# Background work paced by what is needed, a two-part weave of layers 0 and 1, and unread matmuls in the gaps

## The chip, the core and the metric

The kernel runs on one core of a Trainium2 chip. TensorE (PE) multiplies, and its weight loads (PEld) are shown as a row of their own; ScalarE (ACT) applies functions such as exp; VectorE (DVE) works elementwise; GpSimd (POOL) does small jobs; SyncE (SP) issues the DMAs. The metric is the device time of one execution in microseconds, lower is better. Before the change the median of 7 runs is 2521.17 us (2514.41 to 2530.74).

## The reference

Four attention layers follow each other on 2,048 tokens of width 640, with 32 heads of 20. Layers 0 and 2 (weights A) look back over a window of 256 keys, layers 1 and 3 (weights B) over all keys:

```python
def _A_ref(x, wqkv, wo):                     # _B_ref: the same without the mask
    q, k, v = split_heads(x @ wqkv)          # 32 heads of 20
    scores = einsum("bhqd,bhkd->bhqk", q, k) * (Dh ** -0.5)
    mask = (i - j >= 0) & (i - j < 256)
    p = softmax(where(mask, scores, -1e9))
    return merge_heads(einsum("bhqk,bhkd->bhqd", p, v)) @ wo

x = A_x
x = x + _A_ref(_layernorm(x), A_wqkv, A_wo)
x = x + _B_ref(_layernorm(x), B_wqkv, B_wo)
x = x + _A_ref(_layernorm(x), A_wqkv, A_wo)
x = x + _B_ref(_layernorm(x), B_wqkv, B_wo)
```

## The kernel before, in words

The tokens are cut into four chunks of 512 queries (`c`), the heads into eight groups of four (`g`). A *unit* is the attention of one layer, chunk and group. Its scores are made in *banks*: 128 keys by 512 queries of one head, which fill one PSUM bank. A full unit has 64 banks (16 blocks of keys, four heads), a windowed one 12. A *tile* is two or three banks, and the main loop goes through the tiles of all units in the order of the list `units`. For tile `t` it emits:

1. the score matmuls on TensorE (L790), 32 rows each, into one of two PSUM buffers of three banks, so that four heads' strips can run side by side;
2. exp on ScalarE (L804), which writes `pt`;
3. background work, by `pump` (L203);
4. the mask for tile `t-1` on VectorE (L828), in windowed units;
5. the value matmuls (L843) for four banks of two or three tiles earlier, 21 columns of weights each, summed in bank 7 (`op`). At a unit's end VectorE copies `op` away (L668) and a *tail* divides by the sum of the softmax (L685 to L718).

Tiles of units that `narrow` names (layer 0, and the "a" parts of layer 1) alternate between three and two banks, all others have three. While there are narrow units (`state["early"]`) background work has two PSUM banks, 5 and 6; after that only bank 6.

Background work is everything else: layer norm and its transposes (`t_ln`), values (`t_v`), queries and keys (`t_qk_window` for layers 0 and 2, `t_qk_full` for 1 and 3), the output projection (`t_out`). These are Python generators in a list `todo`, sorted by the unit that first needs them. Each yields the cost of what it has just emitted, in *credits*, which are meant as microseconds of TensorE: 0.22 for a matmul of 512 columns, 0.14 for one of 320. A projection is five such matmuls, an output item eight; once begun, an item is emitted whole (`"hold"`), even if credit turns negative, and then nothing is emitted until credit is above zero. Tails come before everything and don't wait for credit. `pump` adds 1.2 credits a tile in layer 0 and 0.6 later, and keeps at most 1.0.

If a unit starts and something it needs isn't made, `require` (L233) emits it at once, however long it takes. The order of instructions on every engine is thus fixed when the program is built; TensorE, ScalarE, VectorE and SyncE each run theirs in that order.

Layers 1 and 3 keep queries, keys and values in DRAM. A projection is evacuated into `st` by VectorE (by ScalarE while `state["act"]`, that is in layer 0), stored, and loaded again as `kt`, `vt`, `qt` by `load_unit` (L592), one unit ahead where its needs are ready. The weights of a group's query and key, padded to 32 rows a head, are one tile `wqk` (320 KB), loaded by `get_w` from DRAM for each chunk, with one load ahead (`take_w`).

The units of layer 1, chunk 0 are cut in "a" (key blocks 0 to 11) and "b" (12 to 15) for the first three groups; part "a" leaves its sum in `raw_o`, and "b" adds to it. They follow all of layer 0. Later, the windowed units of layer 2 are woven between the full units of layers 1 and 3, and layer 3's chunk 0 is cut in the same way for all eight groups.

Of the kernel before, what the change touches and what calls it, by code (L numbers as in the profile page):

```python
# [9 lines left out]
BF16 = mybir.dt.bfloat16  # L10
# [4 lines left out]
P = 128  # L15
# [12 lines left out]
VW = DH + 1  # L28


@with_exitstack
def kernel(
# [19 lines left out]
    wqkp = pool("wqkp", 4)  # L52
# [101 lines left out]
    class Task:  # L154
# [4 lines left out]
        def __init__(self, name, gen, need):  # L159
            self.name, self.gen, self.need, self.wake = name, gen, need, 0  # L160
            self.holds = False
            Task.count += 1
            self.key = (need, Task.count)
# [4 lines left out]
    def push(name, gen, need):  # L168
        insort(todo, Task(name, gen, need))

    def push_tail(name, gen):
        tails.append(Task(name, gen, 0))
# [4 lines left out]
    def advance(task):  # L177
        state["running"] = task
        try:
            kind, n = next(task.gen)  # L180
        except StopIteration:
            drop(task)
            state["held"] = None
            return 0.0
        state["held"] = task if kind == "hold" else None
        if kind == "wait":
            task.wake = state["tick"] + n
            return 0.0
        return n
# [13 lines left out]
    def pump(credit):  # L203
        state["credit"] = min(state["credit"] + credit, 1.0)
        while True:
            t = choose(state["credit"] <= 0.0)
            if t is None:
                break
            state["credit"] -= advance(t)
# [36 lines left out]
    cap = {"qa": 3, "ka": 18, "va": 10, "xnT": 5, "kt": 3, "vt": 3, "qt": 4, "ln": 1, "w": 2, "vs": 2}  # L246

    def room(*tags):
        while any(live[t] >= cap[t] for t in tags):
            yield ("wait", 1)  # L250
        for t in tags:
            live[t] += 1
        state["running"].holds = True
# [16 lines left out]
    worder = {0: [], 1: [], 2: [], 3: []}  # L270

    def get_w(w, g, first):
        t = wqkp.tile([P, 2, KD, P], BF16, name="wqk", tag="wqk")
        if first:
            tv = t[:].rearrange("p n c (j m) -> p (n c) j m", j=4)
            nc.gpsimd.memset(tv[:, :, :, DH:32], 0.0)
            for n in range(2):
                src = raw[:, :, n * D + 80 * g : n * D + 80 * (g + 1)]
                nc.vector.tensor_copy(
                    out=t[:, n].rearrange("p c (j m) -> p c j m", j=4)[:, :, :, 0:DH],  # L280
                    in_=src.rearrange("p c (j e) -> p c j e", j=4),
                )
            nc.sync.dma_start(out=wqk_d[w][g], in_=t[:].rearrange("p n c m -> p (n c m)"))
        else:
            nc.sync.dma_start(out=t[:].rearrange("p n c m -> p (n c m)"), in_=wqk_d[w][g])
        return t

    def push_proj(key, l, w, g, gen, need, first=False):
        worder[l].append((key, w, g, first))
        push(key, gen, need)  # L290

    def take_w(key, l):
        yield from room("w")
        order = worder[l]
        i = next(n for n, e in enumerate(order) if e[0] == key)
        if key not in wtiles:
            wtiles[key] = get_w(*order[i][1:])
            if not order[i][3]:
                yield ("wait", 4)
        i = next(n for n, e in enumerate(order) if e[0] == key)  # L300
        order.pop(i)
        wt = wtiles.pop(key)
        if i < len(order) and not any(e[0] in wtiles for e in order):
            wtiles[order[i][0]] = get_w(*order[i][1:])
        return wt
# [8 lines left out]
    def project(wt, n, xt, dst):  # L314
        mb = yield from take_m()
        pq = ps[:, mb, :]
        for dc in range(KD):
            nc.tensor.matmul(  # L318
                pq, lhsT=wt[:, n, dc, :], rhs=xt[:, dc, :],
                start=(dc == 0), stop=(dc == KD - 1),  # L320
            )
            if dc < KD - 1:
                yield ("hold", 0.22)
        evac(dst(), pq)
        drop_m(mb)
        yield ("pe", 0.22)
# [14 lines left out]
    def t_ln(l, c):  # L341
# [3 lines left out]
        users[l, c] = 10 if l == 1 else 9  # L345
# [95 lines left out]
    def t_qk_window(key, l, c, g):  # L441
        while ("xnT", l, c) not in ready:
            yield ("wait", 1)
        yield from room("qa", "ka")
        wt = yield from take_w(key, l)
        q = qap.tile([P, C], BF16, name="qa", tag="qa")
        yield from project(wt, 0, xnT[l, c], lambda: q[:])
        k = kap.tile([P, C], BF16, name="ka", tag="ka")
        yield from project(wt, 1, xnT[l, c], lambda: k[:])
        live["w"] -= 1  # L450
        qa[c, g], ka[c, g] = q, k
        used(l, c)
        ready.add(("qk", l, c, g))

    def t_qk_full(key, l, c, g):

        while "prep_b" not in ready:
            yield ("wait", 1)
        while ("xnT", l, c) not in ready:
            yield ("wait", 1)  # L460
        wt = yield from take_w(key, l)
        for n, dst in ((1, k_d[l][:, g, c * C : (c + 1) * C]), (0, q_d[l][:, c, g, :])):
            yield from project(wt, n, xnT[l, c], staged)
            nc.sync.dma_start(out=dst, in_=staging.pop())
        live["w"] -= 1
        used(l, c)
        ready.add(("qk", l, c, g))
# [36 lines left out]
    def push_layer(l, c):  # L504

        need = [first_use(l, c, g) for g in range(G)]
        push(("ln", l, c), t_ln(l, c), need[0])
        if l == 1:
            push(("v", l, c, 0), t_v(l, c, (0,)), need[0])
            push(("v", l, c, 1), t_v(l, c, (1,)), need[4])  # L510
        else:
            push(("v", l, c), t_v(l, c, (0, 1)), need[0])
        for g in range(G):
            key = ("qk", l, c, g)
            if l % 2:
                push_proj(key, l, 1, g, t_qk_full(key, l, c, g), need[g])
            else:
                push_proj(
                    key, l, 0, g, t_qk_window(key, l, c, g), need[g], first=(l == 0 and c == 0)
                )  # L520


    class Unit:
        def __init__(self, l, c, g, part=None):
            self.l, self.c, self.g, self.part = l, c, g, part
            self.windowed = l % 2 == 0
            if self.windowed:
                sets = [(m, b0, subs, j) for m, b0, subs in window_banks(c) for j in range(4)]
            else:
                kcs = {None: range(NT), "a": range(12), "b": range(12, NT)}[part]  # L530
                sets = [(None, 0, [(kc, 0, 4, 0)], j) for kc in kcs for j in range(4)]
            n = len(sets)
            self.banks = [
                (self, j, m, b0, subs, i < 4, i >= n - 4, i == n - 1)
                for i, (m, b0, subs, j) in enumerate(sets)
            ]
# [33 lines left out]
    units = [Unit(0, c, g) for c in range(NC) for g in range(G)]  # L570
    units += [Unit(1, 0, g, "a") for g in range(3)]
    units += [Unit(1, 0, g, "b" if g < 3 else None) for g in range(G)]
# [12 lines left out]
    def first_use(l, c, g):  # L585

        if l % 2 == 0:
            return index[l, c, g, None]
        keys = [(l, 0, g, "a" if c < NC - 1 else "b"), (l, 0, g, None)]
        return next(index[k] for k in keys if k in index)  # L590

    def load_unit(u):  # L592
# [3 lines left out]
        k0, k1 = {None: (0, NT), "a": (0, 12), "b": (12, NT)}[u.part]  # L596
# [13 lines left out]
    def unit_needs(u):  # L610
# [3 lines left out]
        chunks = range(NC - 1) if u.part == "a" else range(NC)  # L614
        return [n for cc in chunks for n in (("qk", l, cc, g), ("v", l, cc, g // 4))]
# [69 lines left out]
    def t_tail(l, c, g, on, oT):  # L685
# [36 lines left out]
        if g == G - 1:  # L722
            need = first_use(l + 1, c, 0) if l < 3 else len(units) + c
            push(("out", l, c), t_out(l, c), need)
# [8 lines left out]
    def t_prep_b():  # L733
# [5 lines left out]
        for g in range(G):  # L739
            get_w(1, g, True)  # L740
            yield ("wait", 4)
        ready.add("prep_b")

    with tc.manual_schedule():
        push("stats", t_stats0(0), 0)
# [9 lines left out]
        tiles = []  # L755
        n = 0
        while n < len(banks):
            size = 2 if len(tiles) % 2 and narrow(banks[n][0]) else 3
            tiles.append(banks[n : n + size])
            n += size  # L760

# [3 lines left out]
        for t in range(len(tiles) + 8):  # L765
            state["tick"] += 1
            n_b = 0
            if t < len(tiles):
                cur = tiles[t]
                n_b = len(cur)  # L770
                for b in cur:
                    u = b[0]
                    if id(u) not in started:
                        started.add(id(u))
                        if u.l == 0 and u.g == 0 and u.c + 1 < NC and u.c not in pushed:
                            pushed.add(u.c)
                            push(("stats", u.c + 1), t_stats0(u.c + 1), index[0, u.c + 1, 0, None])
                            push_layer(0, u.c + 1)
                            if u.c == 0:
                                push("prep_b", t_prep_b(), index[0, 1, G - 1, None])  # L780
                        state["unit"] = index[u.l, u.c, u.g, u.part]
                        state["act"] = u.l == 0
# [29 lines left out]
                pump(1.2 if cur[0][0].l == 0 else 0.6)  # L812
            else:
                pump(2.0)
# [37 lines left out]
        while tails or todo:  # L852
            state["tick"] += 1
            pump(5.0)
# [30 lines left out]
```

The softmax here doesn't subtract the row's maximum and nothing guards it: scores larger than these inputs give would overflow.

## Time and profile before

| | before |
|---|---|
| median of 7 runs | 2521.17 us (2514.41 to 2530.74) |
| the profiled execution | 2521.89 us |
| its span, first to last instruction | 2520.2 us |
| TensorE clock granted, mean | 0.736 of full |
| exp on ScalarE, L804 | 1,688 instructions, 2198.6 us busy |
| score matmuls, full units, L790 | 4,096, 716.9 us busy |
| value matmuls, full units, L843 | 4,096, 535.6 us busy |
| query and key projections, L318 | 1,280 issued, 347.8 us busy |
| output projections, L482 | 1,024, 179.6 us busy |
| DMA queue of SyncE | 150.64 MB, 19.3% of 16 engines |

The busy table gives for each engine the time in which it had an instruction, its share of the span and the number of instructions. The row PEclk cuts the span in 40 equal slices (63 us each) and gives the clock that TensorE was granted, in tenths of full speed. The sums by stretch give the same busy times for a chosen window. The chain of waits follows the work that ended last back in time: start, length, what. In the timeline a row is a run of like instructions on one engine; brackets give the idle time before it and what ended it. A matmul's shape such as `32*128 32x512` is rows and columns of weights, then the moving operand.

### The profile page before, as it was taken

Reading aid. Unit: us, or ns where it says so; the run is one execution under the profiler, and the core shown is the slowest. Engines: PE = TensorE matmul, PEld = TensorE weight load, DVE = VectorE, ACT = ScalarE, POOL = GpSimd, SP = SyncE. Lnnn points to the kernel's source line nnn. Section 1 sums busy time; section 2 is a strip of 40 time slices with the busy share of each in tenths; the row PEclk is TensorE's granted clock in tenths of the full one; section 3 lists DMA queues with packets and bytes.
Section 4 is the critical chain, followed back from the end, with each engine's and each line's share of the span. In section 5 each row is a group of like instructions: output and inputs, shape, how many; then the busy total and the mean of one; then the engine's idle time right before and its main releaser. Section 6 shows DMA issues by size and latency. Waiting matters only on the chain.

```text
span 2520.2 us, 37403 instructions
## 1 busy us (share of the span) xinstructions
PE 2060.3 (82%) x15313; PEld 731.5 (29%) x15424; DVE 852.6 (34%) x1925; ACT 2264.8 (90%) x1831; POOL 48.3 (2%) x113
## 2 busy tenths in 40 slices
PE   6788987887878898779987888888877787778777
PEld 3334432322322233223332233233322222222222
DVE  6686842321323334334343434643200010001001
ACT  6778866989998999899999989899999999999995
POOL 2000000000000000000000000000000000000000
PEclk9899998885866699757896589868755565556555
DMA  5212133332210132002231033104211010011100
GB/s 163 70 59 63 46 101 100 112 105 68 66 53 17 42 101 97 29 33 51 79 95 43 1 84 97 62 18 117 79 35 49 32 43 32 33 43 48 32 17 11
DMA packets 92893, 153.03 MB, mean 61 GB/s; under 512 B 8881, under 2 KB 59057, under 8 KB 92721
## 3 DMA queue, kind: packets, MB, share of 16 engines
q1 hardware_dynamic: 92720, 150.64, 19.3%
q8 instruction: 120, 1.97, 0.3%
q14 instruction: 53, 0.43, 0.1%
HBM read 120.46 MB, written 30.15 MB: 60 GB/s over the span
## 4 chain that ended last, share of the span: by engine, by line
ACT 47%; PE 28%; issue 14%; DVE 9%; DMA 1%; SPq 0%; ACTq 0%; POOL 0%; DVEq 0%
ACT pt L804 47%; PE ps L318 9%; PE ps L790 6%; PE ps L843 4%; PE ps L405 4%; PE ps L482 4%; DVE pt L828 3%; DVE oT L668 1%; PE ps L369 1%; DVE st L266 1%; DMA wqk<-wqk_d 1%; DVE on L718 1%; DMA qt<-q_d 1%; DVE qa L266 1%; DVE x_sb L490 1%
## 5 line engine op out<-in xcount | busy, mean ns | idle before, releaser
L804 ACT ACTIVATE pt<-ps 128x1536 bf16<-128x1536 f32 (+1 forms) x1688 | 2198.6, 1532 | 188.5 <-PE ps L790 170.3
L790 PE MATMUL ps<-qt,kt 32*128 32x512 bf16 x4096 | 716.9, 507 | 300.6 <-ACT pt L804 267.2
L843 PE MATMUL ps<-pt,vt 128*21 128x512 bf16 x4096 | 535.6, 509 | 6.0 <-DVE oT L668 4.4
L790 PEld LDWEIGHTS <-kt 32*128 32x128 bf16 x4096 | 204.5, 95 | 771.4 <-issue 738.2
L318 PE MATMUL ps<-xnT,wqk 128*128 128x512 bf16 x1169 | 347.8, 416 | 33.5 <-DMA wqk<-wqk_d 7.4
L828 DVE TENSOR_TENSOR pt<-pt,masks 128x1024 bf16<-128x1024 bf16 (+5 forms) x403 | 240.0, 625 | 215.2 <-ACT pt L804 214.8
L668 DVE CAST oT<-ps 128x512 bf16<-128x512 f32 x117 | 80.3, 686 | 505.4 <-PE ps L843 505.0
L843 PEld LDWEIGHTS <-vt 128*21 128x21 bf16 x4096 | 106.1, 91 | 331.8 <-issue 327.7
L482 PE MATMUL ps<-wop,on 128*128 128x320 bf16 x1024 | 179.6, 324 | 10.3 <-DVE x_sb L490 5.1
L318 PEld LDWEIGHTS <-wqk 128*128 128x128 bf16 x1280 | 116.0, 103 | 190.6 <-issue 102.1
L790 PE MATMUL ps<-qa,ka 32*128 32x384 bf16 (+2 forms) x1408 | 133.6, 320 | 31.2 <-ACT pt L804 28.7
L266 DVE CAST st<-ps 128x512 bf16<-128x512 f32 x119 | 82.3, 692 | 208.3 <-PE ps L318 207.9
L490 DVE TENSOR_TENSOR x_sb<-x_sb,ps 128x320 bf16<-128x320 bf16 x128 | 62.0, 484 | 187.0 <-PE ps L482 184.4
L482 PEld LDWEIGHTS <-on 128*128 128x128 bf16 x1024 | 98.1, 104 | 78.7 <-issue 38.0
L405 PE MATMUL ps<-wv,xnT 128*128 128x320 bf16 x640 | 115.2, 319 | 6.6 <-DVE vs L266 2.1
L718 DVE TENSOR_TENSOR on<-oT,ps 128x512 bf16<-128x512 bf16 x128 | 87.6, 684 | 87.9 <-PE ps L714 86.7
L843 PE MATMUL ps<-pt,va 128*21 128x384 bf16 (+2 forms) x1408 | 88.2, 318 | 18.8 <-DVE oT L668 18.1
L695 DVE RECIPROCAL rz<-ps 128x16 f32<-128x16 f32 x128 | 32.8, 257 | 156.5 <-PE ps L690 147.5
L405 PEld LDWEIGHTS <-xnT 128*128 128x128 bf16 x640 | 58.8, 102 | 51.1 <-issue 29.7
L790 PEld LDWEIGHTS <-ka 32*128 32x128 bf16 x1408 | 39.5, 96 | 116.9 <-issue 110.9
L714 PE MATMUL ps<-rT,spread 32*128 32x128 bf16 x512 | 63.1, 256 | 3.2 <-DVE rT L707 2.3
L369 PE MATMUL ps<-ident,xn 128*128 128x128 bf16 x320 | 36.5, 262 | 25.5 <-DVE xn L360 22.6
(50 smaller groups left out, 646.5 us busy)
## 6 DMA issues: line engine op xcount, KB each, us to landing
wqk<-wqk_d SPq DMA_DIRECT2D x120, 320.0 KB
kt<-k_d SPq DMA_DIRECT2D x53, 512.0 KB
vt<-v_d SPq DMA_DIRECT2D x53, 336.0 KB
qt<-q_d SPq DMA_DIRECT2D x75, 128.0 KB
k_d<-st SPq DMA_DIRECT2D x64, 128.0 KB
q_d<-st SPq DMA_DIRECT2D x64, 128.0 KB
v_d<-vs SPq DMA_DIRECT2D x16, 336.0 KB
wqk_d<-wqk SPq DMA_DIRECT2D x16, 320.0 KB
```

Source lines behind the costliest of these rows:

```text
L266: nc.vector.tensor_copy(out=out_, in_=in_)
L318: nc.tensor.matmul(pq, lhsT=wt[:, n, dc, :], rhs=xt[:, dc, :], start=(dc == 0), stop=(dc == KD - 1),)
L405: nc.tensor.matmul(pv, lhsT=xt[:, dc, i * P : (i + 1) * P], rhs=wv_sb[l % 2][:, dc, h * HD : (h + 1) * HD], start=(dc == 0), stop=(dc == K ...
L482: nc.tensor.matmul(yp, lhsT=on[:, g, qb * P : (qb + 1) * P], rhs=wop[:, g, i * HD : (i + 1) * HD], start=(g == 0), stop=(g == G - 1),)
L490: nc.vector.tensor_tensor(out=xv, in0=xv, in1=yp, op=ALU.add)
L668: nc.vector.tensor_copy(out=oT[:], in_=op)
L714: nc.tensor.matmul(zb[:, qb * P : (qb + 1) * P], lhsT=spread4[:, qb, :], rhs=rT[:], start=True, stop=True,)
L718: nc.vector.tensor_tensor(out=on[:, g, :], in0=oT[:], in1=zb, op=ALU.mult)
L790: nc.tensor.matmul(sp[:, i, col * P : (col + qn) * P], lhsT=u.k(kc, j), rhs=u.q(j, q0, qn), start=True, stop=True,)
L804: nc.scalar.activation(out=pt[:, i:k, b0 * P :], in_=sp[:, i:k, b0 * P :], func=ACT.Exp, scale=SCALE,)
L828: nc.vector.tensor_tensor(out=pt_[:, i:k, b0 * P :], in0=pt_[:, i:k, b0 * P :], in1=mv_, op=ALU.mult,)
L843: nc.tensor.matmul(op[32 * j : 32 * j + VW, q0 * P : (q0 + qn) * P], lhsT=u.v(kc, j), rhs=pt[:, i, col * P : (col + qn) * P], start=(first ...
```

## The change

- Layer 1's chunk 0 is cut for all eight groups, with "a" as key blocks 0 to 7 and "b" as 8 to 15 (`SPLIT`). The first four "a" units are woven between the windowed units of layer 0, chunk 3; the other four follow, then the eight "b". Layer 3 is cut as before.
- Query and key are separate tasks in layers 1 and 3, each with its own need: keys by the part that reads them, queries by the unit of their own chunk. The weights are loaded as halves (160 KB), nine buffers in place of four.
- `state["act"]` ends with layer 0's chunk 2: from chunk 3 on VectorE evacuates.
- `pump` gets a rate. In layer 0, chunks 0 to 2, it is 1.2 as before. After that `rate` takes the largest, over the tasks in hand, of the credits left up to a task divided by the tiles until 16 before its unit, at least 0.6 while early and 0.35 after, times 1.1, at most 0.9. Credit is kept up to the rate and 0.1.
- After the early part and until unit (3, 1, 0) starts, `keep_clock` spends credit that is left on matmuls of the identity with a mask, 128 rows by 512 columns, into bank 6; nothing reads them. The built program has 268 of them.

```diff
+SPLIT = {1: 8, 3: 12}
...
-    wqkp = pool("wqkp", 4)
+    wqkp = pool("wqkp", 9)
...
-    def pump(credit):
-        state["credit"] = min(state["credit"] + credit, 1.0)
+    def pump(credit, most):
+        state["credit"] = min(state["credit"] + credit, most)
...
-    def t_qk_full(key, l, c, g):
+    def t_full(l, n, c, g):
...
-        wt = yield from take_w(key, l)
-        for n, dst in ((1, k_d[l][:, g, c * C : (c + 1) * C]), (0, q_d[l][:, c, g, :])):
-            yield from project(wt, n, xnT[l, c], staged)
-            nc.sync.dma_start(out=dst, in_=staging.pop())
+        yield from room("w")
+        wt = yield from take_w(l, n, c, g)
+        yield from project(wt, xnT[l, c], staged)
+        dst = k_d[l][:, g, c * C : (c + 1) * C] if n else q_d[l][:, c, g, :]
+        nc.sync.dma_start(out=dst, in_=staging.pop())
...
+    def keep_clock():
+
+        while state["held"] is None and state["credit"] > 0.2:
+            b = min(mfree, key=mfree.get)
+            if mfree[b][0] > state["tick"]:
+                return
+            nc.tensor.matmul(
+                ps[:, b, :], lhsT=ident[:], rhs=masks[:, 0, :], start=True, stop=True
+            )
+            state["credit"] -= 0.22
...
-    units = [Unit(0, c, g) for c in range(NC) for g in range(G)]
-    units += [Unit(1, 0, g, "a") for g in range(3)]
-    units += [Unit(1, 0, g, "b" if g < 3 else None) for g in range(G)]
+    units = [Unit(0, c, g) for c in range(NC - 1) for g in range(G)]
+    for g in range(G):
+        units.append(Unit(0, NC - 1, g))
+        if g % 2 == 0:
+            units.append(Unit(1, 0, g // 2, "a"))
+    units += [Unit(1, 0, g, "a") for g in range(G // 2, G)]
+    units += [Unit(1, 0, g, "b") for g in range(G)]
...
+        def rate(t):
+
+            u = tiles[t][0][0]
+            if u.l == 0 and u.c < NC - 1:
+                return 1.2
+            done, r = 0.0, 0.6 if state["early"] else 0.35
+            for task in todo:
+                done += max(task.left, 0.0)
+                if task.need < len(units):
+                    r = max(r, done / max(starts[id(units[task.need])] - t - 16, 1))
+            return min(1.1 * r, 0.9)
...
-                        state["act"] = u.l == 0
+                        state["act"] = u.l == 0 and u.c < NC - 1
...
-                pump(1.2 if cur[0][0].l == 0 else 0.6)
+                r = rate(t)
+                pump(r, r + 0.1)
+                if not state["early"] and state["unit"] < index[3, 1, 0, None]:
+                    keep_clock()
```

## The prediction

> **What bounds the kernel now.** I read the busy table and the row of granted clocks first, then the sums by stretch, then the chain of waits where ScalarE stands still.
>
> ```profile
> span 2520.2 us, 37403 instructions
> PE 2060.3 (82%) x15313; PEld 731.5 (29%) x15424; DVE 852.6 (34%) x1925; ACT 2264.8 (90%) x1831; POOL 48.3 (2%) x113
> PEclk9899998885866699757896589868755565556555
> ```
>
> ScalarE's exp is the bound: 90% busy, and idle time on it is the only time to be won. TensorE's clock is at half speed in much of the second part. Three stretches in the sums (columns: length; busy time and count for PE, PEld, DVE, ACT, POOL; granted clock; DMA share and GB/s):
>
> ```profile
> 260.00:320.00 60.00, 54.25 (x571) 25.40 (x577) 48.71 (x115) 51.45 (x60) 4.07 (x7) 1.00 0.18 53
> 318.50:341.60 23.10, 12.76 (x69) 6.25 (x69) 9.60 (x20) 2.22 (x3) 0.38 (x1) 0.84 0.44 135
> 952.00:1006.00 54.00, 47.09 (x390) 17.56 (x393) 22.02 (x42) 52.37 (x39) 0.00 (x0) 1.00 0.33 108
> 1876.00:2038.00 162.00, 126.42 (x777) 33.74 (x774) 12.52 (x35) 162.00 (x122) 0.00 (x0) 0.50 0.12 38
> ```
>
> In the last one ScalarE never stops although the clock is 0.50: 40 score tiles take 53.7 us there, 1.343 us each, the floor. In the first (layer 0, chunk 3) PE is nearly full. In the second ScalarE does nothing for 21 us. The chain of waits tells why (start, length, what):
>
> ```profile
> 324.83 2.30 DMA k_d<-st
> ...
> 328.24 3.31 DMA wqk<-wqk_d
> 331.55 0.45 issue
> 331.99 3.32 PE ps L318 x9
> 335.32 0.02 issue
> 335.34 0.70 DVE st L266
> ...
> 337.40 3.57 DMA qt<-q_d
> 340.96 0.04 issue
> 341.01 0.29 PE ps L790
> ```
>
> The first unit of layer 1 asks for keys of chunk 2 that are not made: weights are waited for, projected, evacuated, stored, loaded back. Elsewhere what costs time is background work met by a half clock. The timeline of ScalarE and of TensorE where a chunk's output projection begins:
>
> ```profile
> 1812.76 5.65 ACT L804 ACTIVATE pt<-ps 128x1536 bf16<-128x1536 f32 x4 [1.41 <-PE ps L790]
> 1809.39 2.31 PE L482 MATMUL ps<-wop,on 128*128 128x320 bf16 x8
> 1812.58 1.26 PE L482 MATMUL ps<-wop,on 128*128 128x320 bf16 x8
> ```
>
> The same eight matmuls take 2.31 us cold and 1.26 us warm, and the cold ones cost exp 1.41 us. Over the trace, full three-bank tiles that carry one item (five or eight wide matmuls, about 1.1 credit) last 2.705 us on average at half clock (19 tiles), 1.470 us at full clock (156), against 1.343 with none. So a cold item costs 1.36 us, a warm one 0.13. About 24 items ran cold from end to end and as many partly.
>
> **What sets the clock.** [...] By the trace what counts is wide matmuls (128 rows, 128 columns of weights): clock changes come in steps of 3.41 us, and of the windows with under 1,200 wide columns 361 of 367 were followed by half clock, with 2,000 to 4,000 columns 220 of 225 by full clock; the switch is near 1,400. [...] 0.385 credit a tile (0.35 times 1.1) is some 890 columns a tile, 2,270 a window: enough if spread evenly. Items are not: one is issued whole (2,560 columns), then credit is negative for two or more tiles.
>
> **Up to the end of layer 0 and the early parts.** Before's tile 254 and after's tile 263 close the same work (657 and 661 banks, 237 and 235 credits of background), so I compare up to there. Before it ends at 498 us.
> - Stalls. ScalarE's gaps at 341.6 and 344.5 (20.9 and 1.9 us) and at 387.7, 424.2, 441.0, 451.1 (5.7, 4.5, 8.1, 2.3) sum to 43.4. The later three belong to "b" units whose keys are made at the moment of use. In the changed order every full unit but the first of layer 1 has its needs made six or more tiles ahead, so these go. The first still asks at its start, for 11 wide matmuls: 2.4 us warm, up to 3.3 for weights, 5.7 for evacuation, store and load as above, less one tile of cover: +10. Weights now come as halves, and eight of those loads are used within one tile of their place in the order (none within two tiles before); I estimate 1 us each, the 2.4 to 3.8 us that TensorE waits for a weight load issued at its use (at 332 and 384 us) less the lead, and half of them fall here: +4. Net -29.
> - Windowed tiles of chunk 3. They take 1.9 us (tiles 120 to 150) with 1.2 credit each and evacuations on ScalarE behind each item. Afterwards 0.67 credit and evacuation on VectorE. Bounds: 1.13 (exp alone) and 1.9; the row nearest is 1.55 at 0.57 credit in chunk 0. I take 1.5: 33.6 tiles x 0.4 = -13. The 26 evacuations moved (about 0.45 us each of ScalarE) are inside this. VectorE takes them at 0.69 us; it was at 48.7 of 60 us there, so this gain is partly at its mercy.
> - Where that work goes: 102 two-and-three-bank "a" tiles at 1.25 us (1.19 at 0.57 credit before) and 7 full ones at 1.41, 138 us, against 58 at 1.2 and 43 at 1.41, 130 us: +8.
> - Before tile 120 the changed order does 5.5 more credits and stops once for 11 matmuls (layer 0, chunk 2, group 4): +8.
>
> Sum: -26.
>
> **From there to the end.** 1,403 tiles in 1,997 us, of which 123 lie above the floor.
> - Spacing of items. The distance to the item before is one or two tiles for 171 of 233 items before and 105 of 236 after; three tiles for 4 and 61; more for the rest (57 and 69). A burst at 0.6 warms the clock with its first item and pays once; at 0.385 each comes alone. Laying both orders on 1.34 us tiles and 3.41 us windows gives 51 items cold or half cold before (the trace's own number) and 63 after, with 23 and 40 cold throughout. 17 more at 1.36: +22. The bounds: none cold (about -50), or all the 61 at distance three (+76).
> - Unread matmuls: 268 in 152 tiles, from tile 338 to 1118. Warm they cost nothing: a tile's own passes take 0.56 us (0.32 for scores, three in four tiles 0.32 for values, from the starts of such passes around 960 us), two more matmuls 0.43, inside 1.343. Cold, they are 0.85 on top of 0.95 (0.54 a pass at 1942 us): about 0.25 a tile too much; a quarter of the tiles would be cold: +8. If all were: +38.
> - Fewer cold tiles with small pieces: -4. Gone: 6.3 us at 1498 (first "a" unit of layer 3) and 4.8 at 1571 (a weight load); new late halves +4: together -7.
> - Layer 3's output projections after (3,1,0) have no unread matmuls and the slower rate; they are in the count of items.
> - The DMAs move the same bytes in twice as many weight transfers (240 for 120). All are issued by SP, at 20% DMA share, ahead of the stores that follow them: nothing, given leads of four tiles or more.
>
> Sum: +19. Exp itself is unchanged (2,161 us before and after by the same rates; 7 more tiles).
>
> Together -7 on a span of 2520.2. The profiled execution took 2521.9 and the median is 2521.2, so I predict **2514 us** for the median.
>
> **Rivals.**
> - A, as worked out: early gain and later loss nearly cancel, 2490 to 2538.
> - B, the clock is held. For: 2,270 columns a window on average. Against: the empty tiles after each item. Then some 40 of the 51 cold items become warm, 1.24 each, -50; with -4, -7 and -26: 2434.
> - C, the other side: items that come alone run cold. A three-tile distance is 4.0 us, longer than a 3.41 us window, and a tail between two makes it five tiles. From A's 63 on, six more cold items at 1.24 bring the time back to that of before; half of the 61 give 2552, all of them 2590. Against: at exactly three tiles a warm item still leaves half of itself in every window.
> - D, the stall only moves: VectorE, with masks and evacuations of chunk 3 in one queue, holds the windowed tiles at 1.9, and late weight halves cost more than 1 us. Then the early gain is about 8 and the time 2532.
>
> **How the numbers follow.** A measurement tells 0.3% (7.6 us) from no change. A 0.44, B 0.11, C 0.27, D 0.18. A gives 0.22 faster, 0.15 same, 0.07 slower; B 0.11 faster; C 0.02 faster, 0.02 same, 0.23 slower; D 0.02, 0.04, 0.12. Faster 0.37, same 0.21, slower 0.42. To hold 8 in 10 the range takes in A and the nearer half of B and of C: 2462 to 2565.
>
> **What would show it.** Right: no exp gap over 12 us after the first 100 us; gaps at 387 to 451 gone; the granted clock near 1.0 in slices that hold the unread matmuls, and 0.5 to 0.8 where items and tails alternate; mean clock above 0.736, about 0.78; exp gaps of 1 us and more behind a cold item, one by one, from 500 us on, some 50 of them. Wrong: a middle part with mean clock above 0.95 and hardly a gap (B); tile times over 1.5 us throughout 640 to 1500 us (C); windowed tiles of chunk 3 at 1.9 us (D); or PE waits for weights of over 3 us more than a few times.

## The result, and the profile after

The changed kernel takes 2515.12 us in the median of 14 runs (2507.45 to 2519.26), beside 2521.17 of the kernel before in 33 runs on the same chip: ratio 0.9969, 95% interval 0.9957 to 0.9982. The profiled execution took 2514.28 us, with a span of 2512.6. The lines of the page of the changed kernel that answer to those shown of before, with the group of exp (L845) and that of the unread matmuls (L533; the trace has records of 235 of the 268):

```profile
span 2512.6 us, 38178 instructions
PE 2048.6 (82%) x15550; PEld 739.3 (29%) x15692; DVE 868.7 (35%) x1956; ACT 2252.5 (90%) x1812; POOL 48.6 (2%) x129
PEclk9899899988898898879888799889765575557556
...
L845 ACT ACTIVATE pt<-ps 128x1536 bf16<-128x1536 f32 (+2 forms) x1695 | 2197.7, 1509 | 192.2 <-PE ps L831 172.5
...
L533 PE MATMUL ps<-masks,ident 128*128 128x512 bf16 x235 | 86.3, 431 | 3.0 <-issue 1.9
```

Exp is still the bound (ScalarE 90% busy) and its own time is unchanged, 2197.7 us for 2198.6. The clock row is higher in its middle, and from slice 31 on nearly what it was. Cut at the same place as in the prediction (before's tile 254, now tile 263), the traces say:

| end of, us | before | after | difference |
|---|---|---|---|
| tile 120 | 256.8 | 259.8 | +3.0 |
| tile 254 / 263 (early part) | 497.9 | 486.6 | -11.3 |
| last exp | 2494.9 | 2489.1 | -5.8 |

So the early part gained 11 us and the rest gave 6 back. Forecast were 26 and 19: the difference of the two was right, neither of the two was. The early part of the kernel before, with the same instructions, ended at 497.9, 499.2 and 502.0 us in three executions (the second and third from runs 4 and 12 below), and that of the changed kernel at 486.6 to 494.5 in four; over these the gain is about 10.

**Where the early gain went.** TensorE's waits from 256 to 500 us (what waited, for what: us in total, times, longest), first in the kernel before, then in the changed one:

```profile
PE ps L790 <- DMA qt<-q_d: 16.3, 4, 5.4
...
PE ps L318 <- DMA wqk<-wqk_d: 6.3, 2, 3.6
```

```profile
PE ps L318 <- DMA wqk<-wqk_d: 18.6, 7, 5.8
...
PE ps L831 <- DMA qt<-q_d: 5.7, 1, 5.7
```

Score matmuls (L790, now L831) wait for loaded queries once instead of four times, as forecast. But projections (L318) wait seven times for halves of weights, where they waited twice for whole ones. The chain of waits around the longest of these waits (start, length, what; L109 loads weights of an output projection, in four parts), and exp's row in the timeline behind it (brackets: idle before, and what ended it):

```profile
421.95 0.31 SPq L109
...
423.50 6.95 DMA wqk<-wqk_d
430.45 0.05 issue
430.50 0.61 PE ps L318
```

```profile
433.46 2.37 ACT L845 ACTIVATE pt<-ps 128x1536 bf16<-128x1536 f32 x2 [6.92 <-PE ps L831]
```

The half's load is issued right behind the four loads, when its projection is already next, and takes 6.95 us to land, where the two other halves shown here take 2.73 and 3.82. From 421.95 to 430.5 us the DMA engines are 69% busy, at 147 GB/s. TensorE waits 5.78 us for it and exp stands still for 6.92. The chain around the second longest shows why a load can be issued so late:

```profile
461.69 0.59 DVE st L269
462.28 1.97 DMA k_d<-st
464.24 0.02 issue
464.26 0.02 SPq L628
464.28 0.03 issue
464.31 0.32 SPq L628
464.62 0.05 issue
464.68 0.42 SPq L630
465.10 0.05 issue
465.15 0.42 SPq L466
465.57 0.04 issue
465.62 0.43 SPq L287
...
468.20 3.82 DMA wqk<-wqk_d
472.02 0.05 issue
472.06 2.31 PE ps L318 x5
```

In this chain SP issues one transfer behind the other, from 464.31 to 468.20 us. At the head of its queue stands the load of a unit's keys (L628), which waits for the landing of the store of the last of them. SP's own waits from 456 to 475 us:

```profile
SPq L466 <- DVE st L269: 2.0, 1, 2.0
SPq L628 <- DMA k_d<-st: 2.0, 2, 1.1
```

This wait is the one of 1.1 us. Before it SP had stood 2.0 us for an evacuation that a store needs, and 0.9 for the landing of an earlier store. Behind the load of the keys (0.32 us) seven transfers are issued one after another, at 0.42 to 0.49 us each, ahead of the half of the weights that TensorE needs next. That half is issued at 468.20, 3.9 us after the keys. TensorE waits 5.34 us, and exp's gap is 7.18.

**The first "a" unit** asks at its start, as the prediction said, at 263 us:

```profile
263.22 2.73 DMA wqk<-wqk_d
265.95 0.45 issue
266.39 1.93 PE ps L318 x4
268.32 0.02 issue
268.35 0.70 DVE st L269
269.05 0.02 issue
269.06 1.70 DMA k_d<-st
270.76 0.02 issue
270.78 0.32 SPq L628
271.10 0.05 issue
271.15 2.72 DMA qt<-q_d
```

Weights, projection, evacuation, store and load follow one another, and exp's gap that ends at 274.7 is 14.88 us. The gap had begun at 259.8: until the weight load is issued, the chain runs through VectorE's steps of a tail (257.81 to 262.83).

**The rest.** Sums by stretch, from 498 to 1500 and from 1500 to 2490 us, before first and then after (length; busy time and count of PE, PEld, DVE, ACT, POOL; clock; DMA share and GB/s):

```profile
498.00:1500.00 1002.00, 832.24 (x6247) 295.44 (x6293) 351.16 (x775) 928.57 (x705) 10.95 (x30) 0.75 0.20 59
1500.00:2490.00 990.00, 801.70 (x5470) 251.81 (x5487) 195.54 (x440) 959.39 (x712) 3.65 (x10) 0.63 0.16 49
```

```profile
498.00:1500.00 1002.00, 831.45 (x6481) 304.93 (x6547) 360.89 (x802) 926.25 (x704) 10.91 (x30) 0.86 0.20 60
1500.00:2490.00 990.00, 794.06 (x5457) 250.27 (x5481) 190.75 (x431) 953.56 (x706) 3.65 (x10) 0.66 0.15 46
```

In the first of them the clock rose from 0.75 to 0.86, and exp's share didn't rise with it (928.57 and 926.25 us busy of 1002). Tile by tile, with the time above exp's floor of 1.343 us a full tile and the clock around the tile (cold: half speed throughout; part: some of it), from the early part's end on. Windowed tiles count by their columns:

| us above the floor (number of tiles) | before | after |
|---|---|---|
| tiles with an item, cold | 38 (27) | 48 (34) |
| tiles with an item, part cold | 27 (21) | 24 (21) |
| tiles with an item, warm | 27 (187) | 35 (181) |
| tiles with unread matmuls | none | 11 (152) |
| small pieces and all others | 33 | 13 |
| sum | 124 | 132 |

Items lose 108 us instead of 92.

### The profile page after: what moved, and what is told of

Same layout as the page of the kernel before. It is cut to its first block, busy times and chain, and to the rows that moved or that the text cites. A ratio compares the mean times of both kernels' runs of the same rounds, so it can differ in the third digit from the quotient of the medians.

```text
span 2512.6 us, 38178 instructions
## 1 busy us (share of the span) xinstructions
PE 2048.6 (82%) x15550; PEld 739.3 (29%) x15692; DVE 868.7 (35%) x1956; ACT 2252.5 (90%) x1812; POOL 48.6 (2%) x129
## 4 chain that ended last, share of the span: by engine, by line
ACT 42%; PE 31%; issue 15%; DVE 9%; DMA 2%; SPq 0%; POOL 0%; another core or an unknown queue 0%; ACTq 0%; DVEq 0%
ACT pt L845 41%; PE ps L318 10%; PE ps L831 7%; PE ps L887 5%; PE ps L484 4%; DVE pt L872 3%; PE ps L405 3%; DMA wqk<-wqk_d 1%; PE ps L533 1%; DVE st L269 1%; PE ps L739 1%; DVE oT L693 1%; PE ps L369 1%; DVE x_sb L492 1%; DVE on L743 1%
## 5 line engine op out<-in xcount | busy, mean ns | idle before, releaser
L845 ACT ACTIVATE pt<-ps 128x1536 bf16<-128x1536 f32 (+2 forms) x1695 | 2197.7, 1509 | 192.2 <-PE ps L831 172.5
L831 PE MATMUL ps<-qt,kt 32*128 32x512 bf16 x4096 | 680.9, 481 | 285.4 <-ACT pt L845 266.8
L887 PE MATMUL ps<-pt,vt 128*21 128x512 bf16 x4096 | 504.0, 478 | 14.1 <-DVE oT L691 4.6
L831 PEld LDWEIGHTS <-kt 32*128 32x128 bf16 x4096 | 197.1, 94 | 727.4 <-issue 708.4
L318 PE MATMUL ps<-xnT,wqk 128*128 128x512 bf16 x1171 | 357.7, 426 | 46.0 <-DMA wqk<-wqk_d 21.3
L872 DVE TENSOR_TENSOR pt<-pt,masks 128x1024 bf16<-128x1024 bf16 (+6 forms) x403 | 239.2, 625 | 148.3 <-ACT pt L845 148.0
L318 PEld LDWEIGHTS <-wqk 128*128 128x128 bf16 x1280 | 118.7, 105 | 215.2 <-issue 114.3
L831 PE MATMUL ps<-qa,ka 32*128 32x384 bf16 (+2 forms) x1408 | 116.8, 282 | 32.4 <-ACT pt L845 28.5
L533 PE MATMUL ps<-masks,ident 128*128 128x512 bf16 x235 | 86.3, 431 | 3.0 <-issue 1.9
L831 PEld LDWEIGHTS <-ka 32*128 32x128 bf16 x1408 | 40.3, 92 | 101.2 <-issue 94.3
```

What stands on the lines that cost most here:

```text
L318: nc.tensor.matmul(pq, lhsT=wt[:, dc, :], rhs=xt[:, dc, :], start=(dc == 0), stop=(dc == KD - 1),)
L533: nc.tensor.matmul(ps[:, b, :], lhsT=ident[:], rhs=masks[:, 0, :], start=True, stop=True)
L831: nc.tensor.matmul(sp[:, i, col * P : (col + qn) * P], lhsT=u.k(kc, j), rhs=u.q(j, q0, qn), start=True, stop=True,)
L845: nc.scalar.activation(out=pt[:, i:k, b0 * P :], in_=sp[:, i:k, b0 * P :], func=ACT.Exp, scale=SCALE,)
L872: nc.vector.tensor_tensor(out=pt_[:, i:k, b0 * P :], in0=pt_[:, i:k, b0 * P :], in1=mv_, op=ALU.mult,)
L887: nc.tensor.matmul(op[32 * j : 32 * j + VW, q0 * P : (q0 + qn) * P], lhsT=u.v(kc, j), rhs=pt[:, i, col * P : (col + qn) * P], start=(first ...
```

## The experiments

Diffs are against the changed kernel, in runs 4 and 12 against the kernel before and in run 10 against run 9. A kernel's ratio is always to the kernel before, timed beside it, with its 95% interval. "Early end" is the end of tile 254 or 263 in the profiled execution. The same early instructions ended at 486.6, 494.5, 490.5 and 488.8 us in four executions, so one trace doesn't place 4 us. Unread matmuls write a bank that the next item overwrites, so with and without them the same is computed.

**1. The unread matmuls taken out.**

```diff
                 pump(r, r + 0.1)
-                if not state["early"] and state["unit"] < index[3, 1, 0, None]:
-                    keep_clock()
```

> The changed kernel without its 268 unread matmuls; nothing else moves, and the output is the same. Theory (items that come alone pay, the unread matmuls give about what they take): some 20 more items run cold from end to end, 25 us, and the 10 us that the unread matmuls cost in cold tiles, with the cold tiles around them, come back: 2505 to 2535 us, mean clock down from 0.79 to about 0.75. Rival B (the unread matmuls are what pays in this change): over 2540 us.

Measured: 2518.89 us (2514.21 to 2522.82), 0.999 [0.9975, 1.0006]. With the 268 unread matmuls it was 2515.12, so they seem to gain about 4 us; the two intervals overlap, and that is not clear of noise. Without them the clock from 498 to 1500 us falls from 0.86 to 0.79. In the two traces the rest is 2001.0 us without and 2002.5 with them, so a single pair of traces doesn't show where the 4 us lie.

**2. Bursts as before, on the new order, without unread matmuls.**

```diff
-                r = rate(t)
-                pump(r, r + 0.1)
-                if not state["early"] and state["unit"] < index[3, 1, 0, None]:
-                    keep_clock()
+                pump(1.2 if cur[0][0].l == 0 and cur[0][0].c < NC - 1 else 0.6, 1.0)
```

> The changed kernel's weave, separate query and key tasks and half weights, but background work paced as before (1.2 credits a tile in layer 0 up to chunk 2, then 0.6, at most 1.0 kept), and no unread matmuls. Theory (the rate of 0.385 spreads the items over single tiles where each pays for a cold clock): bursts return, the items cold from end to end fall from 34 to about 25, and the gain of the weave stands alone: 2470 to 2500 us. Rival (the pacing is what helps, the weave alone brings stalls): over 2515 us.

Measured: 2504.78 us (2498.59 to 2510.12), 0.9936 [0.9915, 0.9957]: 14 us faster than run 1, and between the two forecasts. Runs 1 and 2 differ in the rate and in the credit kept: up to layer 0's chunk 2 only in the credit kept (1.0 here, 1.3 in run 1), behind it in both. By the traces the gain lies in the early part (479.2 for 494.5; the changed kernel's own early part ends at 486.6 to 494.5, so 7 to 15 us), and the rest is equal (2004.0 and 2001.0, items losing 106 us in both). The edit changes the release of work in both parts, so this pair cannot speak for the spacing of items in the rest. Run 12 was made for that.

**3. Unread matmuls in every tile with no item.** Two of them wherever a tile has no wide work, regardless of credit: 750 for 268.

```diff
-        while state["held"] is None and state["credit"] > 0.2:
+        if state["held"] is None and state.get("wide") != state["tick"]:
             b = min(mfree, key=mfree.get)
...
-            nc.tensor.matmul(
-                ps[:, b, :], lhsT=ident[:], rhs=masks[:, 0, :], start=True, stop=True
-            )
-            state["credit"] -= 0.22
+            for _ in range(2):
+                nc.tensor.matmul(
+                    ps[:, b, :], lhsT=ident[:], rhs=masks[:, 0, :], start=True, stop=True
+                )
```

> The changed kernel with two unread matmuls in every tile in which no wide item and no tail piece was emitted (750 in 375 tiles, 268 in 152 in the changed kernel), whatever the credit, over the same extent. If all that is missing is wide work right after an item, nearly all of the 55 cold and half cold items become warm: about 2455 us and mean clock over 0.85. If tiles that hold tails, where none can be emitted, still let the clock fall, and unread matmuls in cold tiles cost what they save: 2500 to 2520 us.

Measured: 2508.86 us (2503.98 to 2526.13), 0.9963 [0.9939, 0.9988]. The clock from the early part's end to tile 1160 is now 0.935 (after: 0.858), and tiles with an item that are cold or partly cold fall from 55 to 26, which lose 35 us in place of 73. But the warm ones, 210, now lose 0.27 us each (after: 0.20, before: 0.14), and the unread matmuls 20 us. So holding the clock, which rival B priced at -50, wins little.

**4. The two unread matmuls of run 3 on the kernel before,** 786 of them.

```diff
+                if not state["early"] and state["unit"] < index[3, 1, 0, None]:
+                    keep_clock()
```

> The kernel before with nothing changed but two unread matmuls in every tile without a wide item or a tail piece, from the end of its early part to unit (3, 1, 0) (786 in all). Theory: mean clock up from 0.74 to about 0.82, some 25 cold items fewer (30 us), some 25 us paid in cold tiles: 2505 to 2525 us, no change. Rival (a warm clock by itself is worth what cold items cost): 2460 to 2480 us.

Measured: 2540.32 us (2536.17 to 2543.71), 1.0081 [1.0057, 1.0105]: 19 us slower, above both forecasts. Its clock row, and its sum from 498 to 1500 us:

```profile
PEclk9999988999998899988999989989855565556555
```

```profile
498.00:1500.00 1002.00, 874.97 (x6807) 319.33 (x6910) 350.15 (x777) 935.69 (x704) 10.94 (x30) 0.93 0.19 58
```

The clock goes from 0.75 to 0.93, and still the kernel is slower. Cold and partly cold items lose 36 us in place of 65. Warm ones lose 61.5 in place of 26.7 (0.30 each in place of 0.14), and tiles with unread matmuls 28, of which 7 are a stall at 1507 us that the kernel before has too, at 1498. A possible reading: after an item exp is late, and TensorE has to catch up in the next tile; two unread matmuls in that tile take the room for it. That reading was tried in run 6.

**5. Two halves of weights ahead, instead of one.** Same buffers.

```diff
-        if i < len(order) and not any(e[0] in wtiles for e in order):
-            wtiles[order[i][0]] = get_w(*order[i][1])
+        for e in order[i : i + 2]:
+            if e[0] not in wtiles and len(wtiles) < 5 and sum(o[0] in wtiles for o in order) < 2:
+                wtiles[e[0]] = get_w(*e[1])
```

> The changed kernel with weight halves loaded up to two ahead of use in each task list, in the same nine buffers (at most five loaded and not yet used); nothing else. Theory (the early gain fell short because weight loads stand late in SyncE's queue, behind a load that waits for a store, and TensorE waits up to 5.8 us for them between 382 and 475 us): exp's gaps of 2.5, 6.9, 1.7, 2.6 and 7.2 us there shrink by some 15 us in all: 2495 to 2504 us. Rival (the loads themselves are slow, beside other transfers, wherever they stand): 2510 to 2520 us with the same gaps.

Measured: 2497.64 us (2494.68 to 2506.96), 0.9911 [0.9882, 0.994]. TensorE's waits from 256 to 500 us:

```profile
PE ps L319 <- DMA wqk<-wqk_d: 8.1, 5, 3.0
PE ps L832 <- DMA qt<-q_d: 5.6, 1, 5.6
```

Waits for weights fall from 18.6 us to 8.1, and the early end moves from 486.6 to 472.2 us. Of exp's gaps of more than 2.5 us between 280 and 500 us one is left, of 4.42 us. The rival, that these loads are slow wherever they stand, does not hold. The late halves thus cost at least 14 us in the trace and 17 in the median, some 10 to 13 more than the forecast's +4.

**6. Unread matmuls kept out of the tile behind an item.** As in run 3, with one tile more of distance: 446 of them.

```diff
-        while state["held"] is None and state["credit"] > 0.2:
+        if state["held"] is None and state.get("wide", -9) < state["tick"] - 1:
```

> The changed kernel with two unread matmuls in each tile without a wide item or tail piece, but not in the tile that follows an item (446, against 750 without that rule). Theory (unread matmuls right behind an item take the room in which TensorE catches up, so that a warm item costs 0.27 us there and 0.17 without them): warm items come down to 0.2 us, 10 to 15 us in all, the clock stays near: 2494 to 2505 us. Rival (without them the clock falls between items): mean clock well under 0.83, cold items as in the changed kernel, 2508 to 2518 us.

Measured: 2499.21 us (2498.85 to 2499.54), 0.9911 [0.9884, 0.9937]: 16 us below the changed kernel and 10 below run 3, with 304 fewer unread matmuls than that. The rest takes 1985.4 us (after: 2002.5, run 3: 1990.9). A warm item costs 0.19 us again, and the unread matmuls 11 for 20 us. The reading of run 4 forecast this, 0.27 falling to 0.2: room behind an item is worth more here than the clock that the matmuls in it would hold. No run took as many unread matmuls out elsewhere, so that the place counts, and not only their number, is not shown by itself.

**7 and 8. Bursts, two halves ahead, with and without unread matmuls.** Run 8 has the edits of runs 2 and 5, run 7 also that of run 6.

```diff
+                pump(1.2 if cur[0][0].l == 0 and cur[0][0].c < NC - 1 else 0.6, 1.0)
...
+        for e in order[i : i + 2]:
+            if e[0] not in wtiles and len(wtiles) < 5 and sum(o[0] in wtiles for o in order) < 2:
```

> The weave with the old pump (1.2 and then 0.6 credits), weight halves loaded two ahead, and two unread matmuls in tiles without an item or tail piece, not right behind an item. If the three add up: 2505 less some 12 for the loads and 15 for cold items, 2472 to 2485 us. If unread matmuls give nothing where items come in bursts: as the same without them, 2488 to 2498 us.

> The same weave, old pump and loads two ahead, without any unread matmul. Theory: 2505 less 12 for the late loads, 2488 to 2498 us, so that what is measured between this and the combined version is what unread matmuls are worth with bursts (0 to 15 us). Rival on the loads: 2503 to 2510 us, no change from the version that loads one ahead.

Measured: 2495.86 us with unread matmuls (0.9899 [0.987, 0.9928]) and 2492.84 without (0.9886 [0.9856, 0.9917]). With bursts, the unread matmuls of run 6 give nothing that can be told. At the needs' rate they are worth 20 (run 6 against run 1).

**9. The needs' rate, two halves ahead, unread matmuls as in run 6.**

```diff
+        if state["held"] is None and state.get("wide", -9) < state["tick"] - 1:
...
+        for e in order[i : i + 2]:
+            if e[0] not in wtiles and len(wtiles) < 5 and sum(o[0] in wtiles for o in order) < 2:
```

> The changed kernel's pacing and weave with weight halves loaded two ahead, and two unread matmuls in tiles without an item or tail piece and not right behind an item. If the two gains are of different places (late loads before 480 us, warm items after) they add up: 2515 less 17 and 16, 2478 to 2487 us. If they overlap: 2492 to 2500 us.

Measured: 2478.29 us (2471.82 to 2491.59), 0.9825 [0.9795, 0.9854]. The gains of runs 5 and 6 add: 17 and 16 make 33, and measured are 37, with an interval of 7 us to either side.

**10. Run 9 with the "a" units woven later.** The first one comes after group 3 of chunk 3 rather than after group 0.

```diff
-        if g % 2 == 0:
-            units.append(Unit(1, 0, g // 2, "a"))
+        if g >= 3 and g != 4:
+            units.append(Unit(1, 0, (0, 0, 0, 0, 0, 1, 2, 3)[g], "a"))
```

> The one before, with the first part of layer 1 woven in after the fourth windowed unit of chunk 3 in place of the first (then after the sixth, seventh and eighth), so that its keys and query are made by then and nothing is asked for at its start. Theory: exp's gap of 14.8 us at 274 us goes, 2466 to 2475 us. Rival (the wait only moves to a later part, or the windowed tiles lose what this gains): 2478 to 2487 us as before.

Measured: 2476.67 us (2474.01 to 2477.93), 0.9832 [0.9809, 0.9855]. That is the fastest median here, 38 us below the changed kernel's, but not told apart from run 9, and between the two forecasts. The chain of waits shows what became of the stall at the first unit:

```profile
286.53 1.68 DMA k_d<-st
288.22 0.02 issue
288.23 0.32 SPq L631
288.55 0.04 issue
288.60 2.77 DMA qt<-q_d
291.36 0.04 issue
291.40 0.29 PE ps L834
```

With this cover the weights and the projection are done in time, but the store and the load back are not. Exp's gaps there are 3.89 and 6.76 us, where one of 13.97 stood in run 9. Most of the stall's length stays, in smaller pieces.

**11. Evacuations of chunk 3 back on ScalarE.**

```diff
-                        state["act"] = u.l == 0 and u.c < NC - 1
+                        state["act"] = u.l == 0
```

> The changed kernel with ScalarE still evacuating background work in chunk 3 of layer 0, as before the change (one part of the change undone). Theory (26 evacuations of some 0.45 us come back onto ScalarE, between the exps of windowed tiles): 2522 to 2532 us, the loss before 490 us. Rival (VectorE, which takes these at 0.69 us beside the masks, holds the windowed tiles just as long): 2512 to 2518 us.

Measured: 2510.64 us (2504.68 to 2518.55), 0.9962 [0.9944, 0.998], which is not told apart from the changed kernel's 0.9969 and lies below both forecasts. A windowed tile of chunk 3 takes 1.45 us so, and 1.36 with VectorE (before: 1.93): over 36 tiles that is 3 us. So moving evacuations gives little. By the counts the gain of that stretch comes from taking background work out of it (0.72 credit a tile for 1.17).

**12. The new rate alone, on the kernel before.** From tile 254 on, and nothing else. `rate` and the sizes of tasks (`left`) are those of the change, without its early branch.

```diff
-                pump(1.2 if cur[0][0].l == 0 else 0.6)
+                if t < 254:
+                    pump(1.2 if cur[0][0].l == 0 else 0.6)
+                else:
+                    r = rate(t)
+                    pump(r, r + 0.1)
```

> The kernel before with one part of the change alone: from tile 254 on (from the end of layer 0 and the early parts), background work is released by the changed kernel's rate (at least 0.35 times 1.1 credit a tile, credit held to that rate plus 0.1) in place of 0.6 with credit held to 1.0. Order of units, weight tiles, evacuations and the first 254 tiles stay as before, and there are no unread matmuls. The distance from one item to the item before becomes 61 at one tile, 53 at two, 59 at three, 62 at more (before: 56, 118, 3, 58; the changed kernel: 52, 53, 61, 70). Theory of the prediction's step on spacing: items that come alone run cold, +22 for items and -4 for small pieces, so about 2539 us, ratio 1.007. Rival: spacing costs nothing by itself, because a cold burst loses as much at its first items as single items lose, so 2514 to 2528 us, ratio 1.000 within 0.003, with the items' loss above the exp floor staying near before's 92 us. Third: the step was right in size and something else of the change (the order, the split weights) wins it back; that would show as the first number here.

Measured: 2538.31 us (2523.5 to 2540.54), 1.0063 [1.004, 1.0086], 19 us slower than the 2519.15 beside it. The page's lines:

```profile
span 2538.8 us, 37411 instructions
...
PEclk9899988895966689877899689869665575557555
```

In the trace the rest takes 2011.6 us, 14.7 more than before. Tiles with an item lose 113 us in place of 92, with 50 cold or partly cold ones in place of 48. The partly cold rise from 27 to 41 us, the warm from 27 to 35. Those cold throughout lose about what they did (37 us for 38), and are no more (23 for 27). The mean clock is higher than before's, 0.756 for 0.736, and the kernel slower: spreading the items keeps TensorE warm for more of the time, but the items themselves don't get cheaper by it.

## Why the prediction was right, step by step

2514 us were forecast, the median is 2515.12. Errors of opposite sign stand behind that.

| step, as the prediction put it | forecast, us | measured, us | from |
|---|---|---|---|
| before tile 120 | +8 | +3 | the two traces |
| stalls of the early part | -29 | -8 | gaps of exp, 43.4 before, 35.7 after |
| windowed tiles and where that work goes | -13 and +8 | -7 together | what the two rows above leave of -11.3 |
| early sum | -26 | -11 | the two traces |
| spacing of items, fewer cold small pieces | +22 and -4 | +19, or +15 in the trace | run 12 |
| unread matmuls | +8 | -4, not clear of noise | run 1 |
| stalls gone, late halves | -7 | -11 gone | gaps at 1498 and 1571 us |
| sum of the rest | +19 | +6 | the two traces |

- **Spacing of items** was right in direction and size, and that is in part luck. The term was 17 more items cold throughout, at 1.36 us. Its count was 63 cold or half cold, 40 of them throughout; the changed kernel shows 55 and 34, and run 12, without unread matmuls, 50 and 23, where the kernel before has 48 and 27 by the same count. The 17 more cold items aren't there. Run 12's 21 us come from partly cold items (27 to 41 us) and from warm ones (27 to 35): a warm item costs 0.19 to 0.20 us at this rate and 0.14 in bursts, which the forecast didn't have.
- **Before tile 120** the two traces give +3. Over three traces of the kernel before's order and six of the changed order (the end of tile 120 at 256.2 and 261.7 us on average) it is about +5.5, nearer to the forecast.
- **Late weight halves** is the early step that failed. The prediction gave eight of them 1 us each, by the tile in which they are put in the order. That is their place in the program, not the time at which SP issues them or their data land. One stood behind four loads of output weights, another behind eight issues, the first of which waited for a store to land, and TensorE waited 5.8 and 5.3 us. The row on DMAs, "nothing, given leads of four tiles or more", left out the halves without such a lead, and the queue is what decides over those. Run 5 takes most of this away and brings the early end to 472.2, 26 us before that of the kernel before, which is the forecast's early sum.
- **The first unit's stall** was forecast at 10 and is 14.88: the weight load, the matmuls, the evacuation, the store and the load back take 10.8 us (263.22 to 274.01), near the 11.4 of the forecast's parts; but no tile covers them, and exp had already stood still for 3.4 us when the weight load was issued.
- **Windowed tiles of chunk 3** were forecast at 1.5 us, and are 1.36. Where the evacuations run, which was thought to hold part of it, makes some 3 us (run 11).
- **Unread matmuls** were taken to cost 8. In tiles they do lose 10.6 us, 9.7 of it in 38 cold and partly cold ones, 0.26 each. That is the step's own figure, though its parts don't give it: 0.85 on top of 0.95 is 0.46 above 1.343, not 0.25. What was left out is what they save elsewhere. Small pieces and empty tiles lose 20 us less than before, 6 of which are the stall at 1498; for the other 14 the forecast had 4. By run 1 the balance is a gain of 4, not clear of noise.
- **What would show it:** one gap of more than 12 us was there after 100 us (14.88 at 274.7), so this sign spoke against the step on stalls. The gaps of 387 to 451 are gone, but others of 6.92 and 7.18 stand at 433 and 476. The mean clock is 0.794 (forecast 0.78). 41 gaps of 1 us or more after 500 us (forecast some 50, before 44). "Near 1.0 in slices that hold the unread matmuls" is wrong: these slices show 7 to 9 tenths.

**The rivals.** B supposed that a held clock is worth 50 us. Held at 0.93 it makes run 3 about 10 us faster than run 1, with intervals that just overlap, and run 4 19 us slower than the kernel before. A held clock alone doesn't set the price of an item; by runs 4 and 6 the work in the tile behind it does too. C needed cold items beyond A's 63, and there are 55; that single items cost more than bursts is true (run 12), at A's size. D is half right: the stall moved, to weights that come late, not to VectorE.

**The clock.** The prediction took the wide matmuls that it counted in the trace, and not PE's busy time, for what the granted clock follows. The runs agree with that: in the changed kernel's stretch from 1876 to 2038 us PE is again busy for 127 of 162 us at a clock of 0.50, with no idle time of more than 0.73 us; of its 778 matmuls there 28 have 128 rows and 128 columns of weights, and 24 of these move 4 columns. And wide matmuls that nobody reads move the clock of the middle part from 0.75 to 0.93 in run 4, where the queue had little idle time to begin with (832 of 1002 us busy).

**What stays open.** The sums of the table's second half close to within 2 us with run 12's +19 (+19 - 4 - 11 = +4, measured +6) and to within 6 with its trace's +15; terms of 4 us are no larger than the spread between executions.

Why the new order with bursts (run 2) is faster before tile 263 is settled only as to where. The end of tile 120 lies at 248.1 to 252.1 us in the three traces with bursts (runs 2, 7 and 8), and at 258.8 to 264.6 in six with the changed kernel's release (after and runs 1, 3, 5, 6 and 9). Almost all of these tiles get 1.2 credits in both, and what differs is the credit kept, 1.0 for 1.3. Up to tile 263 run 2 has issued 183 credits of projections, values and output items, the changed kernel and run 1 199. The 16 left for later don't lengthen the rest (2004.0 and 2001.0 us). At the first "a" unit run 2 pays for having done less, 23.83 us for run 1's 14.85:

```profile
274.93 2.36 ACT L845 ACTIVATE pt<-ps 128x1536 bf16<-128x1536 f32 x2 [23.83 <-PE ps L831]
```

That work left for later is what shortens the early part is argued from these counts. No run changed the credit kept alone.

## What to carry to other kernels

The lead of a prefetch is counted from when its queue can issue it: here one half of weights was issued 3.9 us behind the load of keys at the head of SP's queue, and TensorE waited 5.34 us for it. Find what stands ahead of it in that queue: how many transfers are to be issued first, and whether one of them waits for a store's landing. Before paying for a warm clock, look at what bounds the tile behind the work that it is to speed up: on the changed kernel filler matmuls gained 20 us where they left that tile free and about 10 where they filled it; with work in bursts they gained nothing that could be told where they left it free (run 7), and cost 19 where they filled it (run 4). When a sum comes out right, check its terms: here an error of 15 us in one part and 13 in the other cancelled, and within the second a term of the right size had the wrong items in it.

## What the runs showed of the hardware that was not expected

- A higher mean clock is no sign of a faster kernel: 0.825 at 2540 us (run 4), 0.756 at 2538 (run 12), 0.748 at 2493 (run 8).
- In the chain at 464 us one transfer occupies SP's queue for 0.32 to 0.49 us at its issue; eight in a row ahead of a load delay it by 3.9 us, as much again as its transfer takes (3.82). Behind four loads of 200 KB a transfer of 160 KB took 6.95 us to land.
- The store of a tile, its load back and the start of matmuls on it take 4.9 us (286.53 to 291.40), 1.68 and 2.77 of them in the two transfers; that is most of the 6.76 us gap that is left there in run 10.
